# One gated-mix kernel: a bias loaded once, queries stacked in pairs of blocks, late masks moved to VectorE, and normalized tiles that land where they are split

## The chip, the cores and the metric

The kernel runs on one core of a Trainium2 chip. The metric is the device time in microseconds of one execution, the median of several. The profile names the engines PE (TensorE matmuls), PEld (its weight loads), DVE (VectorE), ACT (ScalarE), POOL (GpSimd) and SP (SyncE, which here issues every DMA).

## The reference, cut to what matters

The input `x` is 2048 rows of 512 floats. Three things are computed from it and mixed per row.

```
g = sigmoid((x * gate_w).sum(-1))                      # one number per row
a = attention(x): qkv = x @ wqkv, 32 heads of 16,      # row q sees rows q-255 .. q
    p = softmax(q.k / 4, masked), o = p @ v, a = o @ wo
b = gelu(x @ w1 + b1) @ w2 + b2                        # 512 -> 1792 -> 512
out = g * a + (1 - g) * b
```

## The kernel before, in words

All large products keep float32 accuracy by a split: each operand is a high part plus a low remainder, and `mm3` (lines 92 to 95) issues three 128x512 matmuls for one product. The high part of a tile is written by ACT (a copy into the F32R type), the remainder by DVE (a subtraction of that copy from the original).

**Order.** Nothing is scheduled by a tool. The program walks a hand-written loop, and `after(ns, fn)` puts later steps into a heap that is ordered by a virtual clock; `tick` advances that clock by each matmul's nominal length. So each engine's instructions stand in a fixed order which constants such as `LANDO`, `HOLD`, `HOLDO`, `NORM` and `DIV` set. At run time an engine works strictly down its list: an instruction that waits holds up everything behind it on that engine. SP issues all DMAs of the program from one such list, and each DMA signals on one of eight semaphores in turn, so a DMA's issue also waits until the one eight places earlier has landed.

**Stages.** First q, k and v are computed for four chunks of 512 rows and stored to DRAM. From then on two strands are interleaved on PE: the attention, and the dense part (MLP and then the output product) that fills the gaps. The attention goes through 8 groups of 4 heads; a group has 16 blocks of 128 keys, so there are 128 units (`u`). A unit that is 12 units ahead (`LEAD`) computes row maxima (`att_max`: matmul `sm` of `qd` and `kd`, L456; masked maximum on DVE, L461); `att_rows` turns four blocks' maxima into extra rows of the query tile `qs` by small POOL copies (`put`, L483). The unit itself computes scores (`st`, L500), exponentials on ACT (`pt`, L515) and clears the masked triangles of `pt` with POOL selects (L506, L509). After every fourth unit `att_pvs` multiplies the exponentials with v (L537): 98 small matmuls, which go through six blocks in pairs, the first pair being the first and the last block. A chunk's result `nd` is added up (L558 ACT, L561 DVE) and stored (L565).

**Stacking.** A tile such as `ks` or `qd` holds two heads' rows, one above the other, for alternating 64-wide column pieces. `ks` already uses pairs: the upper head takes the two middle pieces of every four, the lower head the two outer ones, so most runs are 128 elements long (three DMAs, L415, L410, L412). `qd` alternates single pieces of 64 elements (two DMAs, L429). `qs` receives whole rows (L436).

**Normalization.** For each chunk and each pair of groups `att_norm` loads the sums `den` (L575), takes reciprocals on DVE (L579), stores them (L582), loads them back spread over the heads as `rb` together with `num` (L587), multiplies on DVE (L591) and stores the tile `OT` (L594). `load_o` brings `OT` into a raw tile (L629), ACT writes the high part (L632), DVE the low part (L635), and `final` multiplies with `wo` (PE `a`, L93 to L95), mixes (L802) and stores the output (L807). Numbers behind a name give group or chunk: `nd7_1` is group 7, chunk 1; `num0_3` is chunk 0, pair 3 of groups.

**The bias.** In the first half of the MLP each output block starts from `b2`, loaded and spread over 128 rows by `ya_load` (L679), 16 times; in the second half it starts from the stored first half (L682).

Of the kernel before, what the change touches and what calls it, by code (L numbers as in the profile page):

```python
# [32 lines left out]
def gated_mix(ctx: ExitStack, tc: tile.TileContext, x, wqkv, wo, w1, b1, w2, b2, gate_w, out):  # L33
# [14 lines left out]
    idle = sb.tile([128, 384], BF16, tag="jm", bufs=1, name="idle")  # L48
# [20 lines left out]
    for r in (0, 64):  # L69
        nc.gpsimd.affine_select(out=mask[r:r + 64, 0:64], in_=mask[r:r + 64, 0:64], pattern=[[1, 64]],  # L70
                                compare_op=ALU.is_ge, fill=NEG, base=-1, channel_multiplier=-1)
        nc.gpsimd.affine_select(out=mask[r:r + 64, 256:320], in_=mask[r:r + 64, 256:320], pattern=[[-1, 64]],
                                compare_op=ALU.is_ge, fill=NEG, base=0, channel_multiplier=1)

# [243 lines left out]
    def warm(n):  # L318

        p = ps.tile([128, T], F32, tag="d", bufs=2, name=f"warm{now[0]}")  # L320
        for _ in range(n):
            nc.tensor.matmul(p[:, 0:384], idle[:, 0:128], idle, start=True, stop=True)
            tick(160)
# [76 lines left out]
    def load_ks(g_, c):  # L400


        ready(c, g_, 1)
        n = 2 * NB
        for s in range(2):
            v = f32(ks[64 * s + 4:64 * s + 52, slot(g_, c)]).rearrange("r a x -> r (a x)")
            src = part(SK[c], g_, s)
# [17 lines left out]
    def load_qd(g_, c):  # L425
        ready(c, g_, 0)
        for s in range(2):
            v = f32(qd[48 * s:48 * s + 48, slot(g_, c)]).rearrange("r a (n s j) -> r (a n) s j", s=2, j=64)[:, :, s]
            nc.sync.dma_start(v, part(SQ[c], g_, s).rearrange("r (n j) -> r n j", j=64))  # L429
# [37 lines left out]
    def att_rows(g_, rb):  # L467
# [11 lines left out]
        def put(i):  # L479
            r = 64 * (i // 2)  # L480
            dst = qs[r:r + 4, :, rb * RB * 128:(rb + 1) * RB * 128]
            dst = dst.rearrange("r s (b i j) -> r s b i j", b=2 * RB, i=2)[:, :, :, i % 2]
            nc.gpsimd.tensor_copy(dst, tt[32 * i:32 * i + 4].unsqueeze(1).broadcast_to([4, 2, 2 * RB, 32]))  # L483
            if i == 3:
                done.add(("rows", g_, rb))
        for i in range(4):
            after(PUT * (i + 1), put, i)

    def att_exp(g_, kb, i):
# [13 lines left out]
        def sel():  # L503
            for r in (0, 64):
                v = pt[r:r + 64]
                nc.gpsimd.affine_select(out=v[:, :, 0:64], in_=v[:, :, 0:64], pattern=[[0, 2], [1, 64]],  # L506
                                        compare_op=ALU.is_ge, fill=0.0, base=0, channel_multiplier=-1)
                if w == W + 64:
                    nc.gpsimd.affine_select(out=v[:, :, W:W + 64], in_=v[:, :, W:W + 64],  # L509
                                            pattern=[[0, 2], [-1, 64]], compare_op=ALU.is_ge, fill=0.0, base=-1,  # L510
                                            channel_multiplier=1)
# [9 lines left out]
    def att_pvs(u):  # L521
# [38 lines left out]
        def ev():  # L560
            nc.vector.tensor_add(nd, nd, pv[1])  # L561
            after(HOLD, store)

        def store():
            nc.sync.dma_start(ND[c][g_ // 2][g_ % 2], nd)  # L565
            done.add(("nd", g_, c))
            if g_ % 2 == 1:
                after(NORM, att_norm, c, g_ // 2)
        after(100, half), after(700, ev)

    def att_norm(t, c):

        v = ND[t][c].rearrange("g (i r) c -> (g i) r c", r=32)
        den = sb.tile([128, 32], F32, tag="den", bufs=2, name=f"den{t}_{c}")
# [21 lines left out]
        for ns, fn in zip(DIV, (rcp, keep, back, mul, store)):  # L596
# [16 lines left out]
    def load_o(t, cs=range(NC)):  # L613
# [8 lines left out]
        for c in cs:  # L622
            need(("o", t, c))
            if t == 0:
                raw = sb.tile([128, T], F32, tag=("x1", "raw")[c % 2], bufs=2, name=f"or{t}_{c}")
            else:
                raw = sb.tile([128, 2, 320], F32, tag="pt", bufs=PTS, name=f"or{t}_{c}")
                raw = raw.rearrange("p a b -> p (a b)")[:, 0:T]
            nc.sync.dma_start(raw, OT[t][c])  # L629

            def hi(c=c, raw=raw):
                nc.scalar.activation(ot[c][:, 0], raw, AF.Copy)  # L632

            def lo(c=c, raw=raw):
                nc.vector.tensor_sub(ot[c][:, 1], raw, f32(ot[c][:, 0]))  # L635
                done.add(("ot", t, c))
            n = cs.index(c)
            land = LAND if t == 0 else LANDO
# [33 lines left out]
    def ya_load(k):  # L672
# [3 lines left out]
        half, t = TURNS[n]  # L676
        yas[k] = ya = sb.tile([128, D], F32, tag="ya", bufs=2, name=f"ya{t}_{half}{b}")
        if half == 0:
            nc.sync.dma_start(ya, b2.partition_broadcast(128))  # L679
# [98 lines left out]
    def final(t):  # L778
# [3 lines left out]
        for b in range(NB):  # L782
# [8 lines left out]
            for k in range(n):  # L791
# [16 lines left out]
                after(100, ev), after(100 + HOLDO, store)  # L808
# [35 lines left out]
    for u in range(-LEAD, NU):  # L844
# [39 lines left out]
WARM = (7, 3)  # L884
# [16 lines left out]
LANDO = 5000.0  # L901
HOLD = 4000.0
HOLDQ = 1500.0
HOLDO = 1200.0
DIV = (6000, 9000, 12000, 18500, 22000)
# [26 lines left out]
```

## Time and profile before

| | |
|---|---|
| three timed runs | 787.20, 788.38, 788.43 us (median 788.38) |
| profiled execution | 788.64 us, span of its instructions 786.9 us |
| mean granted TensorE clock | 0.985 |
| busy share | PE 95%, DVE 65%, ACT 55%, POOL 55% |
| DMA | 176.07 MB in 203950 packets; 87.9% of sixteen engines' span |

The span runs from the first to the last instruction. A share of the whole span mixes the stages: up to about 110 us only q, k and v are computed, from 110 to about 735 us attention and MLP are interleaved, and from 735 us only the output product is left. The rows the argument rests on stand in the prediction.

### The profile page before, as it was taken

How to read it: one execution, taken by the hardware profiler on the slowest of the kernel's cores; microseconds unless marked ns; L12 is line 12 of the kernel's file. 1: busy time of each engine (PE TensorE's matmuls, PEld its weight loads, DVE VectorE, ACT ScalarE, POOL GpSimd, SP SyncE). 2: the span in 40 equal slices, each digit the busy share in tenths (PEclk: the TensorE clock that was granted, in tenths of full speed). 3: DMA queues.
4: the chain of work that ended last, by engine and by line, in shares of the span. 5: the costliest groups of instructions: out<-in, count | busy, mean ns of one | idle time of the engine just before them, and what ended most of it. 6: DMA issues, size and time to landing. Idle time of an engine off the chain costs nothing. (4 is left out here: it accounts for less than half of the span.)

```text
span 786.9 us, 18205 instructions
## 1 busy us (share of the span) xinstructions
PE 747.3 (95%) x6102; PEld 616.2 (78%) x6102; DVE 510.5 (65%) x1548; ACT 432.9 (55%) x973; POOL 431.3 (55%) x1129
## 2 busy tenths in 40 slices
PE   8999999979999999999999999999999999977988
PEld 6888887757888887887878777888888888765767
DVE  3532326869758867875897689678758966722434
ACT  4434433249448734854784577458547845943442
POOL 3200000219867964886797679768758966963100
PEclk9999999989999999999999999999999999988999
DMA  9979899998996899899878999996999998347563
GB/s 280 369 250 362 293 349 296 239 282 180 258 252 148 195 244 208 191 205 259 196 170 183 218 241 215 242 228 116 223 226 237 199 246 221 70 109 212 193 234 110
DMA packets 203950, 176.07 MB, mean 224 GB/s; under 512 B 102480, under 2 KB 145744, under 8 KB 203856
## 3 DMA queue, kind: packets, MB, share of 16 engines
q1 hardware_dynamic: 203856, 174.90, 87.9%
q8 instruction: 48, 0.79, 0.5%
q14 instruction: 46, 0.38, 0.2%
HBM read 112.47 MB, written 62.39 MB: 222 GB/s over the span
## 5 line engine op out<-in xcount | busy, mean ns | idle before, releaser
L461 DVE CUSTOM_DVE_ANT_0 jm<-sm,mask 128x320 bf16<-128x320 f32 (+4 forms) x512 | 238.1, 465 | 72.9 <-PE sm L456 44.4
L515 ACT ACTIVATE pt<-st 128x320 f32<-128x320 f32 (+4 forms) x512 | 206.4, 424 | 130.2 <-PE st L500 126.7
L506 POOL TENSOR_SCALAR_AFFINE_SELECT pt<-pt 64x128 f32<-64x128 f32 x512 | 182.6, 357 | 153.7 <-ACT pt L515 131.9
L509 POOL TENSOR_SCALAR_AFFINE_SELECT pt<-pt 64x128 f32<-64x128 f32 x448 | 167.3, 373 | 0.0
L456 PE MATMUL sm<-kd,qd 96*128 96x320 f32 (+4 forms) x512 | 157.3, 310 | 9.9 <-DMA ya<-in_B_b_dram 4.9
L500 PE MATMUL st<-qs,ks 128*128 128x320 f32 (+4 forms) x512 | 156.1, 309 | 7.0 <-ACT pt L515 7.0
L456 PEld LDWEIGHTS sm<-kd,qd 96*128 96x128 f32 x512 | 96.6, 189 | 39.5 <-DVE M L461 15.8
L500 PEld LDWEIGHTS st<-qs,ks 128*128 128x128 f32 x512 | 97.8, 191 | 27.4 <-ACT pt L515 8.7
L483 POOL CAST qs<-tt 4x512 fp32r<-4x512 f32 x128 | 88.4, 691 | 35.3 <-DVE tt L477 16.2
L93 PE MATMUL y<-w,h 128*128 128x512 f32 x224 | 90.7, 405 | 0.0
L94 PE MATMUL y<-w,h 128*128 128x512 f32 x224 | 88.6, 395 | 0.0
L95 PE MATMUL y<-w,h 128*128 128x512 f32 x224 | 88.3, 394 | 0.0
L537 PE MATMUL pv_sm<-pt,vbuf 64*32 64x320 f32 (+4 forms) x1408 | 82.5, 366 | 5.6 <-DVE M L461 3.5
L537 PE MATMUL pv_st<-pt,vbuf 64*32 64x320 f32 (+4 forms) x1408 | 80.9, 366 | 6.7 <-POOL pt L506 3.9
L93 PE MATMUL u<-mx,w 128*128 128x512 f32 x196 | 80.1, 409 | 0.0
L537 PEld LDWEIGHTS pv_sm<-pt,vbuf 64*32 64x32 f32 x1408 | 60.0, 112 | 23.7 <-DVE M L461 6.3
L94 PE MATMUL u<-mx,w 128*128 128x512 f32 x196 | 77.3, 394 | 0.0
L95 PE MATMUL u<-mx,w 128*128 128x512 f32 x196 | 77.1, 393 | 0.0
L537 PEld LDWEIGHTS pv_st<-pt,vbuf 64*32 64x32 f32 x1408 | 54.1, 112 | 7.6 <-POOL pt L506 4.2
L299 POOL MEMSET vx<- 128x32 f32 x16 | 2.5, 156 | 93.1 <-DMA SK<-qke 32.0
L280 DVE TENSOR_TENSOR qke<-qk,qke 128x512 fp32r<-128x512 f32 x32 | 22.1, 690 | 46.6 <-ACT qke L277 36.6
L95 PEld LDWEIGHTS y<-w,h 128*128 128x128 f32 x224 | 42.3, 189 | 10.0 <-DVE h L665 0.2
(140 smaller groups left out, 1341.3 us busy)
## 6 DMA issues: line engine op xcount, KB each, us to landing
kd<-SK SPq DMA_DIRECT2D x32, 384.0 KB
qd<-SQ SPq DMA_DIRECT2D x64, 192.0 KB
qs<-SQ SPq DMA_DIRECT2D x64, 192.0 KB
mx<-XT SPq DMA_DIRECT2D x24, 512.0 KB
SQ<-qke SPq DMA_DIRECT2D x16, 512.0 KB
SK<-qke SPq DMA_DIRECT2D x16, 512.0 KB
ND<-nd SPq DMA_DIRECT2D x32, 256.0 KB
raw_w<-in_B_w_dram SPq DMA_DIRECT2D x28, 256.0 KB
```

Of the source, the lines that this page charges most:

```text
L93: nc.tensor.matmul(p, lh, rh, start=first, stop=False)
L94: nc.tensor.matmul(p, lh, rl, start=False, stop=False)
L95: nc.tensor.matmul(p, ll, rh, start=False, stop=last)
L280: nc.vector.tensor_sub(e[:, 1 - h], p, f32(e[:, h]))
L456: nc.tensor.matmul(p[:, :w], qd[0:96, n, pr, 128 * j:128 * (j + 1)], kd[0:96, n, pr, k1 - w:k1], start=True, stop=True)
L461: nc.vector.tensor_tensor_reduce(junk[:, :w], p[:, :w], mask[:, 320 - w:320], 1.0, -3e38, ALU.add, ALU.max, M[:, 2 * (b % RB) + hb, pr:pr ...
L483: nc.gpsimd.tensor_copy(dst, tt[32 * i:32 * i + 4].unsqueeze(1).broadcast_to([4, 2, 2 * RB, 32]))
L500: nc.tensor.matmul(p[:, :w], ks[:, slot(g_, kb // NB), pr, at:at + 128], qs[:, pr, k0:k0 + w], start=True, stop=True)
L506: nc.gpsimd.affine_select(out=v[:, :, 0:64], in_=v[:, :, 0:64], pattern=[[0, 2], [1, 64]], compare_op=ALU.is_ge, fill=0.0, base=0, channel ...
L509: nc.gpsimd.affine_select(out=v[:, :, W:W + 64], in_=v[:, :, W:W + 64], pattern=[[0, 2], [-1, 64]], compare_op=ALU.is_ge, fill=0.0, base=- ...
L515: nc.scalar.activation(pt[:, pr, :w], p[:, :w], AF.Exp, scale=SCALE)
L537: nc.tensor.matmul(pv[r // 64][32 * i:32 * i + 32, q - c * T:e - c * T], vts[g_, b // NB][r:r + 64, v:v + 32], rhs(r), start=start, stop=s ...
```

## The change

Five things change.

1. `b2` is loaded once; the one tile serves all sixteen blocks.
2. `qd` is stacked in pairs like `ks`, through a shared `put_pairs`: three DMAs a load instead of two, with runs of 128 elements in place of 64. The query rows that `put` writes follow the new stacking, so each of its copies is cut in two (256 of 256 elements a row in place of 128 of 512).
3. In the last 12 units the masks are one DVE minimum with a constant tile `cut` (3e38 where a value is kept, zero where it is masked) per half block, in place of two or four POOL selects.
4. `load_o` loads `OT` straight into the low half of the tile that is split; ACT reads it there and DVE overwrites it. The raw tiles fall away; the load itself now waits until the tile's former user is done.
5. Delays: the first query loads `load_qs(0, ...)` come at every fourth unit, `LAND0` is 13500 for the first chunk's split (7500 before), `LANDO` 6500 (5000), `HOLDO` 3000 (1200), and the last two normalizations use shorter delays. The warm-up matmuls are 9 of 320 columns in place of 7 of 384.

The core of the diff:

```diff
+    cut = cp.tile([128, 2, 64], F32, name="cut")
+    nc.gpsimd.memset(cut, 3e38)
...
+        put_pairs([f32(ks[64 * s + 4:64 * s + 52, slot(g_, c)]) for s in range(2)], SK[c], g_)
+
+    def put_pairs(to, st, g_):
...
     def load_qd(g_, c):
         ready(c, g_, 0)
-        for s in range(2):
-            v = f32(qd[48 * s:48 * s + 48, slot(g_, c)]).rearrange("r a (n s j) -> r (a n) s j", s=2, j=64)[:, :, s]
-            nc.sync.dma_start(v, part(SQ[c], g_, s).rearrange("r (n j) -> r n j", j=64))
+        put_pairs([f32(qd[48 * s:48 * s + 48, slot(g_, c)]) for s in range(2)], SQ[c], g_)
...
-            nc.gpsimd.tensor_copy(dst, tt[32 * i:32 * i + 4].unsqueeze(1).broadcast_to([4, 2, 2 * RB, 32]))
...
+            src = tt[32 * i:32 * i + 4].rearrange("r (b h) j -> r b h j", h=2)[:, :, hb]
+            nc.gpsimd.tensor_copy(dst, src.unsqueeze(1).broadcast_to([4, 2, RB, 32]))
...
+            if g_ * NKB + kb >= NU - LEAD:
+                v = pt.rearrange("p a (e x) -> p a e x", x=64)[:, :, 0:4 * n - 3:4]
+                nc.vector.tensor_tensor(v, v, cut[:, 0:n].unsqueeze(1).broadcast_to([128, 2, n, 64]), op=ALU.min)
...
-            after(HOLD, store)
+            after(HOLD if g_ * NT + c < NQ - 2 else 800, store)
...
-                after(NORM, att_norm, c, g_ // 2)
+                after(NORM if g_ * NT + c < NQ - 2 else 3500, att_norm, c, g_ // 2)
...
-        for ns, fn in zip(DIV, (rcp, keep, back, mul, store)):
+        for ns, fn in zip(DIVS[c == NC - 1 and t >= NT - 2], (rcp, keep, back, mul, store)):
...
-            nc.sync.dma_start(raw, OT[t][c])
+            nc.sync.dma_start(f32(ot[c][:, 1]), OT[t][c])
...
-                nc.scalar.activation(ot[c][:, 0], raw, AF.Copy)
+                nc.scalar.activation(ot[c][:, 0], f32(ot[c][:, 1]), AF.Copy)
...
-            land = LAND if t == 0 else LANDO
+            land = LAND0 if t == 0 else LANDO
...
+        if half == 0 and k:
+            yas[k] = xts["b2"]
+            return
...
-        if QAT <= m < QAT + NT - 1:
-            load_qs(0, m - QAT)
-        if m == QAT + NT:
-            load_qs(0, NT - 1)
+        if m % NB == QAT % NB and QAT <= m < QAT + NKB:
+            load_qs(0, (m - QAT) // NB)
...
-LANDO = 5000.0
+LAND0 = 13500.0
+LANDO = 6500.0
...
-HOLDO = 1200.0
-DIV = (6000, 9000, 12000, 18500, 22000)
+HOLDO = 3000.0
+DIVS = ((6000, 9000, 12000, 18500, 22000), (4500, 5700, 8500, 13500, 15000))
```

Where the order moves, the changed file's own line numbers stand in the rows. First, VectorE near the end of the attention, around the normalization of chunk 0; before the change:

```order
L733 SCALAR_TENSOR_TENSOR yo_10623<-y3_11_10571,ya3_11_9962 128x512
L591 TENSOR_TENSOR num0_3_10642<-num0_3_10642,rb0_3_10644 128x512
L579 RECIPROCAL den1_3_10659<-den1_3_10659 128x32
L635 TENSOR_TENSOR ot0_10661<-or0_0_10662,ot0_10661 128x512
L635 TENSOR_TENSOR ot0_10661<-or0_1_10664,ot0_10661 128x512
L635 TENSOR_TENSOR ot0_10661<-or0_2_10666,ot0_10661 128x512
L561 TENSOR_TENSOR nd7_2_10774<-nd7_2_10774,pv7_2_sm_10720 128x512
```

The same place with the change (L520 is the new minimum, L607 the multiply, L646 the low part of a split):

```order
L748 SCALAR_TENSOR_TENSOR yo_10722<-y3_11_10679,ya3_11_10092 128x512
L607 TENSOR_TENSOR num0_3_10738<-num0_3_10738,rb0_3_10740 128x512
L595 RECIPROCAL den1_3_10752<-den1_3_10752 128x32
L520 TENSOR_TENSOR pt7_11_1_10749<-pt7_11_1_10749,cut_151 128x2x2x64
L520 TENSOR_TENSOR pt7_12_0_10777<-pt7_12_0_10777,cut_151 128x2x2x64
L577 TENSOR_TENSOR nd7_2_10851<-nd7_2_10851,pv7_2_sm_10797 128x512
L646 TENSOR_TENSOR ot0_10754<-ot0_10754 128x512 x2
```

The three splits of chunk 0 have moved from ahead of the sum `nd7_2` to behind it, and the mask of the last block of group 7's third chunk (`pt7_11_1`) now stands on VectorE behind the multiply of `num0_3`.

Second, the DMA list of SP around the first query loads of the attention, before the change:

```order
L436 DMA qs_174<-SQ1_71 48x2x512 x2
L145 DMA raw_w20_1545<-in_B_w2_dram 128x512
L284 DMA SK3_77<-qke3_6_1535 128x2x512
L285 DMA SK3_77<-qke3_6_1535 128x512
L436 DMA qs_174<-SQ2_72 48x2x512 x2
L423 DMA kd_177<-SK2_76 96x2x256
L423 DMA kd_177<-SK3_77 96x2x512
L429 DMA qd_176<-SQ3_73 48x16x64 x2
```

And with the change (L428, L423 and L425 are the three DMAs of a paired load, L436 is now `kd`):

```order
L153 DMA raw_w20_1558<-in_B_w2_dram 128x512
L292 DMA SK3_77<-qke3_6_1548 128x2x512
L293 DMA SK3_77<-qke3_6_1548 128x512
L436 DMA kd_183<-SK2_76 96x2x256
L436 DMA kd_183<-SK3_77 96x2x512
L428 DMA qd_182<-SQ3_73 48x8x128
L423 DMA qd_182<-SQ3_73 48x7x128
L425 DMA qd_182<-SQ3_73 48x2x64
```

The four loads of `qs` for chunks 1 and 2, which stood ahead of the maxima's `kd` and `qd` for chunk 3, now come later, and one `qd` load is three DMAs with longer runs.

More of the change, by code (lines that the diff above doesn't have):

```diff
@@ L46, in f32 @@
         return ap.bitcast(F32)
-    idle = sb.tile([128, 384], BF16, tag="jm", bufs=1, name="idle")
+    idle = sb.tile([128, 320], BF16, tag="jm", bufs=1, name="idle")
     nc.gpsimd.memset(idle, 0.0)
@@ L321, in warm @@
         for _ in range(n):
-            nc.tensor.matmul(p[:, 0:384], idle[:, 0:128], idle, start=True, stop=True)
-            tick(160)
+            nc.tensor.matmul(p[:, 0:320], idle[:, 0:128], idle, start=True, stop=True)
+            tick(134)
     def qkv(t):
@@ L573, in att_norm @@
         v = ND[t][c].rearrange("g (i r) c -> (g i) r c", r=32)
-        den = sb.tile([128, 32], F32, tag="den", bufs=2, name=f"den{t}_{c}")
+        den = sb.tile([128, 32], F32, tag="den", bufs=1, name=f"den{t}_{c}")
         nc.sync.dma_start(den, v[:, 16, :].rearrange("i (j c) -> i j c", c=32))
@@ L807, in store @@
                     nc.sync.dma_start(out[nb * 128:(nb + 1) * 128, cs], a[:, cs])
-                after(100, ev), after(100 + HOLDO, store)
+                after(100, ev), after(100 + (HOLDO if nb < NT * NB - 2 else 800), store)
     later = [("w1", i) for i in range(HF)] + [("w2", i) for i in range(HF)]
```

51 lines of the change are left out of this document (27 added, 24 removed).

## The prediction

> **What bounds the kernel now.** I read the page's busy shares first, then PE's waits, then windows around them.
>
> ```profile
> PE 747.3 (95%) x6102; PEld 616.2 (78%) x6102; DVE 510.5 (65%) x1548; ACT 432.9 (55%) x973; POOL 431.3 (55%) x1129
> DMA packets 203950, 176.07 MB, mean 224 GB/s; under 512 B 102480, under 2 KB 145744, under 8 KB 203856
> q1 hardware_dynamic: 203856, 174.90, 87.9%
> ```
>
> PE works 95% of the span and the change takes no matmul of the product away, so all it can win lies in the 39.6 us in which PE idles and in matmuls that ran at a lowered clock. The DMA engines, 88% busy, are the second resource. Who ended PE's waits, in us, times, longest:
>
> ```profile
> PE st L500 <- ACT pt L515: 7.0, 4, 5.5
> PE sm L456 <- DMA ya<-in_B_b_dram: 4.9, 1, 4.9
> PE pv_st L537 <- POOL pt L506: 3.9, 2, 3.4
> PE a L93 <- DVE ao L802: 3.5, 2, 2.0
> ```
>
> Four places make up half of the idle time: one at the attention's start, two in its last chunks, one in the output product. Windows (length, busy PE, PEld, DVE, ACT, POOL, then the granted clock, DMA share, GB/s) show what comes on top:
>
> ```profile
> 166.00:175.00 9.00, 5.49 (x18) 4.79 (x19) 6.22 (x19) 4.84 (x10) 0.82 (x2) 0.62 0.91 320
> 624.80:627.50 2.70, 2.70 (x98) 2.11 (x97) 2.34 (x9) 1.03 (x2) 2.53 (x7) 1.00 1.11 241
> 689.90:698.70 8.80, 5.19 (x98) 3.67 (x97) 1.54 (x3) 1.65 (x4) 5.38 (x16) 0.65 0.07 11
> 717.20:722.30 5.10, 4.96 (x98) 3.57 (x97) 0.00 (x0) 0.51 (x2) 1.83 (x7) 0.50 0.69 182
> 732.10:735.60 3.50, 3.00 (x99) 2.23 (x97) 0.69 (x1) 0.95 (x2) 0.79 (x3) 1.00 0.19 57
> 735.50:787.00 51.50, 44.59 (x210) 36.56 (x204) 21.79 (x34) 17.32 (x28) 0.00 (x0) 1.00 0.53 180
> ```
>
> The same 98 matmuls of `att_pvs` take 2.7 us at full clock (group 6, chunk 1) and 8.8 us for group 7, chunk 1, where a wait of 3.4 us was followed by half clock. For chunk 2 they take 5.1 us at half clock behind a wait of 5.5 us. Waits of that length are paid for twice.
>
> **The change part by part.** Sums are made against the profiled execution (span 786.9, time 788.64, so 1.7 us lie around the span; its time is 0.3 above the median of 788.38).
>
> *The attention's start.* The wait, a window around it, SP's list (start, length) and the sizes:
>
> ```profile
> 169.51 0.64 PE L456 MATMUL sm<-kd,qd 96*128 96x320 f32 x1 [4.94 <-DMA ya<-in_B_b_dram]
> 164.00:170.00 6.00, 1.06 (x5) 0.62 (x4) 1.50 (x4) 2.30 (x4) 0.00 (x0) 0.75 1.01 271
> 154.49 2.15 SPq L436 DMA_DIRECT2D qs<-SQ  x2
> 156.73 0.97 SPq L423 DMA_DIRECT2D kd<-SK  x2
> 157.75 1.01 SPq L429 DMA_DIRECT2D qd<-SQ  x2
> 164.28 2.08 SPq L679 DMA_DIRECT2D ya<-in_B_b_dram  x2
> qd<-SQ SPq DMA_DIRECT2D x64, 192.0 KB
> ya<-in_B_b_dram SPq DMA_DIRECT2D x16, 256.0 KB
> ```
>
> The wait of 4.9 us is named after `ya`, but the matmul reads `kd` and `qd`, issued at 156.7 to 158.8 and, if the last of them ended the wait at 169.5, landed some 11 us later: the DMA queue is backed up, its engines busy throughout (1.01). Four `qs` loads of 192 KB that stood ahead now come later: 0.79 MB at the 320 GB/s of the window are 2.5 us. Four paired `qd` loads stand ahead or are the awaited one: 1536 runs each become 816. For a run's price I have two bounds: at one price per byte nothing is won; at the mean price per packet, 0.879 x 786.9 x 16 / 203856 = 54 ns, 4 x 720 x 54 / 16 ns = 9.7 us. I take a third, 3.2 us, because half-length packets cannot cost as much as the mean of all. 2.5 + 3.2 = 5.7 exceeds 4.9, so the wait goes, and with it the low clock: 9.00 x (1 - 0.62) = 3.4 us, less the 1.2 of it that fall into the wait (6.00 x 0.25 = 1.5 up to 170.0). **-7.1**, bounds -2.5 (the `qs` loads alone) and -7.1.
>
> The Trainium skill ("DMA: Bandwidth & Descriptors", section "Specifications") says that transfers under 512 B miss line rate, because the engine reads, modifies and writes. By that rule halving the number of runs pays, and the sum is the -17.7 below; were bytes the only price, this term would be -2.5 and the sum -13.1. No row of this profile tells the two apart.
>
> *The rest of the DMA relief.* Fifteen loads of `b2`, 3.9 MB, at the mean 224 GB/s are 17.6 us of queue time; 28 more `qd` loads bring 0 to 68 (at 54 ns a run). Neither is on PE's path as such. What it shortens are VectorE's waits for `rb`:
>
> ```profile
> L591 DVE TENSOR_TENSOR num<-num,rb 128x512 f32<-128x512 f32 x16 | 11.2, 701 | 22.2 <-DMA rb<-RD 21.0 <-issue 1.3
> 300.00:450.00 150.00, 144.16 (x1349) 121.01 (x1348) 114.98 (x371) 93.55 (x213) 107.94 (x283) 0.99 0.91 205
> ```
>
> PE idles 5.8 us in this window. I take **-1.5** for the whole middle, bounds 0 and -6. SP gets 32 - 15 = 17 issues more of about 0.5 us; it waits far more than it issues.
>
> *The masks of the last chunks.* A DVE operation on two tiles of 128x512 floats takes 0.69 us (713.61 in the rows below), a minimum over half as many about 0.36, and one replaces four selects. For chunk 1 the wait goes, 8.8 - 2.7 = 6.1; VectorE gets eight minima (3 us) among GELU steps, so I keep 0.5 of delay: **-5.6**, bounds -3 and -6.1.
>
> *Chunks 2 and 3* have another cause, and the price is worked out from chunk 1's end (698.7):
>
> ```profile
> 700.05 0.34 DVE L579 RECIPROCAL den<-den 128x32 f32<-128x32 f32 x1
> 700.18 0.44 ACT L515 ACTIVATE pt<-st 128x320 f32<-128x320 f32 x1 [0.76 <-PE st L500]
> 703.60 0.61 SPq L587 DMA_DIRECT2D rb<-RD  x1
> 713.61 0.69 DVE L591 TENSOR_TENSOR num<-num,rb 128x512 f32<-128x512 f32 x1 [4.34 <-DMA rb<-RD]
> 714.22 2.07 ACT L632 ACTIVATE ot<-or 128x512 fp32r<-128x512 f32 x3 [5.06 <-DMA or<-OT]
> 716.67 0.63 PE L500 MATMUL st<-qs,ks 128*128 128x320 f32 x1 [5.45 <-ACT pt L515]
> 730.01 0.69 DVE L591 TENSOR_TENSOR num<-num,rb 128x512 f32<-128x512 f32 x1 [3.08 <-DMA rb<-RD]
> ```
>
> Before, ACT stood at the split `ot<-or`, waiting for its DMA, and the exponentials queued behind it. Now that split comes behind chunk 2's product, and ACT is free. But the product's first pair needs the mask of block 11, which stands on VectorE behind the multiply `num`, and that waits for `rb`: 713.61, 14.9 after chunk 1's end. It even comes 0.9 later, since the reciprocal now stands behind a mask that needs the exponential of 700.18. So chunk 2 can start at 14.9 + 0.9 + 0.7 (multiply) + 0.35 + 0.36 = 17.2. PE arrives at 711.2 - 698.7 = 12.5 plus 0.3 for a score, 12.8, and waits 4.4: longer than the 3.4 us that halved the clock at chunk 1, so the 5.1 us of before again: end at 22.3 (before 23.6). The next multiply follows 16.4 after the first (730.01 - 713.61), at 32.2; behind it stand three masks, a `yo` and the mask of block 15: 0.7 + 0.7 + 4 x 0.2 = 2.2, so 34.4. PE arrives 9.8 (732.1 - 722.3) after 22.3, at 32.1, and waits 2.3. With 2.7 - 0.3 for the product, the output product starts 36.8 after chunk 1's end: before 735.5 - 698.7 = 36.8. **0**: the ACT wait is exchanged for a VectorE wait. Bounds: -8.8 if the multiply is never late (12.8 + 2.7 + 9.8 + 2.7 = 28.0), +4 if both waits halve the clock.
>
> *The output product:*
>
> ```profile
> 761.92 0.23 PE a L94
> 754.23 0.50 PE L93 MATMUL a<-wo,ot 128*128 128x512 f32 x1 [2.04 <-DVE ao L802]
> 751.60 1.90 DVE L635 TENSOR_TENSOR ot<-or,ot 128x512 fp32r<-128x512 f32 x3 [0.96 <-ACT ot L632]
> 745.70 1.35 SPq L629 DMA_DIRECT2D or<-OT  x3
> 750.93 1.84 ACT L632 ACTIVATE ot<-or 128x512 fp32r<-128x512 f32 x3 [8.83 <-DMA or<-OT]
> ```
>
> VectorE stood at a split whose tile had not landed, the mix `ao` behind it came late, and PE found no free PSUM. Later splits (`LANDO`) and output stores that no longer hold up SP (`HOLDO`) take both waits away: **-3.5**, bounds 0 and -3.5. The new condition, that `OT` of chunk 2 may land only when chunk 0's product is done, leaves chunk 1's product, 48 matmuls of 0.23 us = 10.9 us, for a load that took 5.2 (745.70 to 750.93) and four subtractions (2.8): hidden by 2.9; without that cover, 1 to 2 us.
>
> *Costed at nothing:* `put` and the warm-up.
>
> ```profile
> L483 POOL CAST qs<-tt 4x512 fp32r<-4x512 f32 x128 | 88.4, 691 | 35.3 <-DVE tt L477 16.2 <-PE sm L456 11.9
> 8.19 0.50 PE L93 MATMUL qk<-ks,qk 128*128 128x512 f32 x1 [0.72 <-ACT qk L153]
> ```
>
> Twice as many copies of half the size cost POOL between 0 and 88 us more in all, 0 to 2.8 us for each set of four that becomes eight; POOL is 55% busy and the rows are made some units ahead of their use, which covers it. Without that cover each of 32 sets could delay scores by up to 2.8. The warm-up (some 0.2 us longer) ends in a wait for ACT.
>
> Sum: -7.1 - 1.5 - 5.6 + 0 - 3.5 = -17.7; span 769.2, time **770.9**.
>
> **The rivals.**
>
> *VectorE's multiply is in time* (0.22). The DMA queue, with 23040 fewer of 102480 small packets, brings `rb` before PE arrives at chunks 2 and 3. For it: `rb` was issued 10 us before it landed, so queueing is most of it. Against it: the bytes ahead of it in this stretch (`YB`, `num`, 2 KB rows) are unchanged. -17.7 - 8.8 = -26.5: 762.1.
>
> *The queue is not relieved* (0.15). Run length is no price, or another transfer takes the place of the awaited one, and output waits reappear elsewhere: -2.5 at the start, 0 in the middle, -5.6, +2 at chunks 2 and 3, 0 at the end: -6.1, 782.5. This is also the case in which the change does not do what it says.
>
> *SP becomes the bound* (0.05), slower than before. Each paired load puts a third DMA, of 24 KB only, into the list, and every issue waits for the landing of the one eight places earlier; in the backlog two issues took 2.15 us (154.49). If each of the 32 loads holds SP a further 1.1 us and `kd`, `qd` reach PE that much later, 35 - 9.1 (masks and output product) = +26, 814; it decides from the point at which SP's lead over PE is used up, and only what exceeds 9.1 makes the kernel slower. Against it: of the four waits listed above only the one at 169.5 is for such a load. The Trainium skill ("DMA: Bandwidth & Descriptors", section "Bandwidth") calls transfers under 64 KB dominated by their descriptors, which speaks for this rival; it measured loads issued by GpSimd, and no run here shows it yet.
>
> **How the numbers follow.** Forecast 0.58, rivals 0.22, 0.15, 0.05. The time is the forecast's, 771. Its own range is 765 to 777, from the bounds at the start, for the masks and at chunks 2 and 3; with most of the in-time case and of the unrelieved one it becomes 761 to 783. Differences under 0.2%, 1.6 us, cannot be told from none; the unrelieved case ends there at times: faster 0.92, same 0.03, slower 0.05.
>
> **What would show it.** The page of the changed kernel should show about 46000 fewer packets under 512 B (`qd`'s 32 x 1536 runs become 32 x 816, of which 96 each stay short) and DMA share below 88%; PE's wait for `sm` at 165 to 170 gone; chunk 1's 98 matmuls in under 3.5 us; at chunk 2 a PE wait of 3 to 5 us with VectorE at `num` before it; no wait of `a` for `ao`. A PE wait for POOL in the last 100 us, or for `kd` or `qd` in the middle, would prove me wrong; so would chunk 2 without a wait, in the other direction.

## The result and the profile after

The changed kernel takes 778.14 us (median of 775.01, 777.76, 778.52 and 778.56), the kernel before 787.79 us beside it. The ratio is 0.9872 with a 95% interval of 0.9841 to 0.9903: 1.3% faster, 9.7 us. The forecast was 771, in a range of 761 to 783. The profiled execution took 778.52 us, with a span of 776.8. One execution of `e11_v` below took 1015.32 us at a mean granted clock of 0.655, a slow state that is in neither its median nor its ratio.

The rows of the changed kernel's page that answer to those shown of before: busy shares, DMA packets, the DMA queue.

```profile
PE 744.8 (96%) x6104; PEld 615.8 (79%) x6104; DVE 515.9 (66%) x1572; ACT 431.6 (56%) x973; POOL 424.6 (55%) x1174
DMA packets 179262, 172.14 MB, mean 222 GB/s; under 512 B 56672, under 2 KB 122976, under 8 KB 179168
q1 hardware_dynamic: 179168, 170.97, 83.4%
```

The runs under 512 B fell by 45808, as forecast, and the DMA engines' share from 87.9 to 83.4%. PE still idles 32 us. Who ended its waits (us, times, longest):

```profile
PE pv_st L553 <- POOL pt L525: 4.4, 5, 1.7
PE sm L467 <- DVE M L472: 3.7, 7, 1.0
PE pv_st L553 <- issue: 3.5, 1, 3.5
PE a L101 <- DVE ao L817: 3.1, 2, 2.3
PE pv_st L553 <- DVE pt L520: 2.3, 1, 2.3
```

In the first row the waits for POOL's masks have moved. The kernel before had three at `pv_st`, two at L506 (3.9 us, in the prediction) and one at L509:

```profile
PE pv_st L537 <- POOL pt L509: 1.3, 1, 1.3
```

The longest of these, 3.4 us, was the chunk 1 of group 7 that the masks were moved for. After the change there are five, none of them in the last 100 us. Windows around the same places as before (columns as there), the three middle ones being the products of chunks 1, 2 and 3 of group 7:

```profile
166.00:175.00 9.00, 6.85 (x30) 5.30 (x31) 8.04 (x26) 6.54 (x15) 4.76 (x11) 0.97 1.10 288
...
687.59:690.07 2.48, 2.48 (x97) 2.05 (x96) 2.29 (x5) 1.62 (x4) 0.00 (x0) 1.00 0.17 24
702.33:709.88 7.55, 4.00 (x97) 2.92 (x96) 1.56 (x4) 0.44 (x1) 0.00 (x0) 0.81 0.61 177
719.54:724.47 4.93, 2.61 (x98) 2.03 (x96) 2.36 (x7) 1.35 (x3) 0.00 (x0) 1.00 0.63 220
724.47:776.80 52.33, 46.03 (x211) 37.68 (x204) 21.95 (x35) 17.08 (x28) 0.00 (x0) 0.97 0.53 177
```

Split at the products (each stage ends where the next matmul starts), in us:

| stage | before | after | change | forecast |
|---|---|---|---|---|
| up to the first attention product | 190.5 | 187.4 | -3.1 | -7.1 |
| the middle, up to the end of group 7, chunk 0 | 486.2 | 486.4 | +0.2 | -1.5 |
| to the end of chunk 1 | 22.0 | 16.2 | -5.7 | -5.6 |
| chunks 2 and 3 | 36.8 | 34.4 | -2.4 | 0 |
| output product | 51.4 | 52.3 | +0.9 | -3.5 |
| span | 786.9 | 776.8 | -10.1 | -17.7 |

One warning for what follows. Eight kernels here (the changed one and runs `e2`, `e4`, `e7`, `e8`, `e10`, `e11`, `e12` below) have the same middle, and in their single profiles it takes from 483.3 to 488.6 us. So a stage of one profile speaks for a cause only where a wait or a product shows it; whole kernels are compared by ratios, whose intervals are some 0.25 to 0.45% to each side.

### The profile page after: what moved, and what is told of

The parts are those of the page before. It is cut to its first block, busy times and chain, and to the rows that moved or that the text cites. A ratio compares the mean times of both kernels' runs of the same rounds, so it can differ in the third digit from the quotient of the medians.

```text
span 776.8 us, 18309 instructions
## 1 busy us (share of the span) xinstructions
PE 744.8 (96%) x6104; PEld 615.8 (79%) x6104; DVE 515.9 (66%) x1572; ACT 431.6 (56%) x973; POOL 424.6 (55%) x1174
## 3 DMA queue, kind: packets, MB, share of 16 engines
q1 hardware_dynamic: 179168, 170.97, 83.4%
## 4 chain that ended last, share of the span: by engine, by line
PE 65%; DMA 13%; POOL 6%; DVE 6%; issue 3%; SPq 3%; ACT 3%; DVEq 0%; ACTq 0%; POOLq 0%
PE sm L467 7%; PE st L513 6%; PE pv_sm L553 6%; POOL pt L525 5%; DMA rb<-RD 5%; PE y L101 5%; PE u L101 4%; PE y L103 4%; PE y L102 4%; PE u L103 4%; PE u L102 4%; PE qk L101 4%; PE qk L103 3%; PE qk L102 3%; PE v L101 2%
## 5 line engine op out<-in xcount | busy, mean ns | idle before, releaser
L525 POOL TENSOR_SCALAR_AFFINE_SELECT pt<-pt 64x128 f32<-64x128 f32 x872 | 294.1, 357 | 102.7 <-ACT pt L531 82.0
L495 POOL CAST qs<-tt 4x256 fp32r<-4x256 f32 x256 | 116.9, 457 | 39.1 <-DVE tt L488 15.6
L553 PE MATMUL pv_st<-pt,vbuf 64*32 64x320 f32 (+4 forms) x1408 | 76.8, 355 | 12.2 <-POOL pt L525 4.4
L553 PE MATMUL pv_sm<-pt,vbuf 64*32 64x320 f32 (+4 forms) x1408 | 78.7, 355 | 2.4 <-DVE M L472 1.2
L553 PEld LDWEIGHTS pv_sm<-pt,vbuf 64*32 64x32 f32 x1408 | 56.3, 108 | 19.9 <-DVE M L472 3.1
L553 PEld LDWEIGHTS pv_st<-pt,vbuf 64*32 64x32 f32 x1408 | 50.5, 108 | 13.4 <-POOL pt L525 7.3
L574 ACT ACTIVATE nd<-pv_st 128x512 f32<-128x512 f32 x32 | 19.1, 597 | 57.5 <-PE pv_sm L553 53.4
```

The lines of the kernel that those rows point to most:

```text
L495: nc.gpsimd.tensor_copy(dst, src.unsqueeze(1).broadcast_to([4, 2, RB, 32]))
L525: nc.gpsimd.affine_select(out=v, in_=v, pattern=[[0, 2], [1 - 2 * e, 64]], compare_op=ALU.is_ge, fill=0.0, base=-e, channel_multiplier=2 * ...
L553: nc.tensor.matmul(pv[r // 64][32 * i:32 * i + 32, q - c * T:e - c * T], vts[g_, b // NB][r:r + 64, v:v + 32], rhs(r), start=start, stop=s ...
L574: nc.scalar.activation(nd, pv[0], AF.Copy)
```

## The experiments

Each run changes the kernel after the change, unless it says otherwise; all ratios are to the kernel before, timed beside it on the same chip. As a yardstick: the change itself is 0.9872.

| run | what | median, us | ratio, 95% interval |
|---|---|---|---|
| `e1_single` | `qd` in single pieces again | 779.20 | 0.9898 (0.9852 to 0.9943) |
| `e2_poolmask` | last masks on POOL again | 783.75 | 0.9960 (0.9933 to 0.9987) |
| `e3_split` | kernel before, row copies cut in two | 791.75 | 1.0050 (1.0022 to 1.0078) |
| `e4_chunk1` | VectorE masks for chunk 1 only | 775.89 | 0.9863 (0.9819 to 0.9908) |
| `e5_qs` | first `qs` loads where they were | 783.43 | 0.9947 (0.9921 to 0.9972) |
| `e6_b2` | `b2` loaded sixteen times | 781.88 | 0.9918 (0.9887 to 0.9949) |
| `e7_land` | `LANDO`, `HOLDO` as before | 774.58 | 0.9847 (0.9806 to 0.9888) |
| `e8_mul` | three multiplies on POOL | 772.21 | 0.9805 (0.9776 to 0.9834) |
| `e10_raw` | `e4`, own buffers for the last `nd` | 776.94 | 0.9866 (0.9831 to 0.9902) |
| `e11_v` | `e10`, last v loaded early | 777.34 | 0.9869 (0.9824 to 0.9914) |
| `e12_all` | `e11`, two multiplies on POOL | 774.95 | 0.9835 (0.9794 to 0.9876) |
| `e14_dve` | `e12`, chunk-1 masks on VectorE in all groups | 766.56 | 0.9742 (0.9703 to 0.9780) |

**The middle: what the paired stacking gives and takes.** Two runs separate its two halves, the shorter DMA queue and the smaller POOL copies. The first takes both back, the second puts the smaller copies alone into the kernel before.

```diff
 e1_single
-        put_pairs([f32(qd[48 * s:48 * s + 48, slot(g_, c)]) for s in range(2)], SQ[c], g_)
+        for s in range(2):
+            v = f32(qd[48 * s:48 * s + 48, slot(g_, c)]).rearrange("r a (n s j) -> r (a n) s j", s=2, j=64)[:, :, s]
+            nc.sync.dma_start(v, part(SQ[c], g_, s).rearrange("r (n j) -> r n j", j=64))
...
+            nc.gpsimd.tensor_copy(dst, tt[32 * i:32 * i + 4].unsqueeze(1).broadcast_to([4, 2, 2 * RB, 32]))
 e3_split (on the kernel before)
-            nc.gpsimd.tensor_copy(dst, tt[32 * i:32 * i + 4].unsqueeze(1).broadcast_to([4, 2, 2 * RB, 32]))
+            src = tt[32 * i:32 * i + 4].rearrange("r (b h) j -> r b h j", h=2)[:, :, hb]
+            nc.gpsimd.tensor_copy(dst, src.unsqueeze(1).broadcast_to([4, 2, RB, 32]))
```

> The changed kernel with one part undone: qd is stacked in single pieces of 64 again (two DMAs a load) and each row copy on POOL is whole again (4 of 512 elements in place of 8 of 256). Theory (in the middle, the smaller copies on POOL cost as much as the shorter DMA queue gives): POOL copies about 690 ns each, 88 us in all, in place of 117; the chunk-1 products of groups 0, 3 and 4 take 2.9 to 3.2 us again in place of 4.6, 4.6 and 6.2; the wait of about 5 us for kd, qd at the attention's start and PE's waits behind longer rb waits return; the middle stays within 2 us of 486.3, the start is 2 to 4 us longer, so 780 to 783 us in all. Rival (the row copies do not matter, the DMA relief is simply worth little): the products of chunk 1 stay at 4.5 us and more, and the whole is within 1 us of 778.1, or 3 us up at the start alone. Rival (the paired loads cost more than they give): 774 or less.

> The kernel before with one thing changed: each row copy on POOL is cut into two of half the size (8 of 256 elements in place of 4 of 512), same stacking and same DMAs as before. Theory (the smaller copies are what lengthens chunk 1's products in the middle): copies of about 457 ns, 117 us in all; the chunk-1 products of several groups take 1 to 3 us longer than the 2.6 to 3.1 us of before, and the whole is 3 to 9 us above the kernel before. Rival (POOL has room for the copies; the products of the changed kernel are longer for another reason): within 1 us of the kernel before, products unchanged.

The product of group 3, chunk 1, shows it in one window of each trace. After the change, then `e3_split`, `e1_single`, and `e14_dve`, of which more below:

```profile
408.89:413.47 4.58, 2.90 (x96) 2.15 (x96) 3.33 (x10) 0.95 (x2) 4.22 (x12) 1.00 0.98 188
```

```profile
416.34:420.92 4.58, 2.90 (x97) 2.15 (x97) 3.33 (x10) 1.07 (x3) 4.25 (x13) 1.00 1.26 193
```

```profile
410.42:413.48 3.06, 2.71 (x96) 2.12 (x96) 2.78 (x9) 0.95 (x2) 2.83 (x8) 1.00 1.28 218
```

```profile
406.68:409.10 2.42, 2.42 (x96) 1.99 (x96) 1.78 (x7) 0.87 (x2) 1.75 (x5) 1.00 1.23 189
```

PE's work is about the same each time; the rest is waiting while POOL (the fifth pair of numbers) works without a pause. With small copies the window is 4.58 us, whatever the stacking (4.58 to 6.28 in the eight kernels of the same middle); with whole copies it is 3.06, and before the change it was 3.07. Groups 4 and 6 go the same way (6.23 and 3.74 us after the change, 3.06 and 2.58 in `e1_single`), group 5 by 0.3 only. POOL's copies in the changed kernel (count, busy time, mean ns of one) and its list ahead of that window (start, length):

```profile
L495 POOL CAST qs<-tt 4x256 fp32r<-4x256 f32 x256 | 116.9, 457 | 39.1 <-DVE tt L488 15.6
...
376.77 3.86 POOL L495 CAST qs<-tt 4x256 fp32r<-4x256 f32 x6
380.70 1.59 POOL L525 TENSOR_SCALAR_AFFINE_SELECT pt<-pt 64x128 f32<-64x128 f32 x4
382.35 0.40 POOL L495 CAST qs<-tt 4x256 fp32r<-4x256 f32 x1
382.81 12.63 POOL L525 TENSOR_SCALAR_AFFINE_SELECT pt<-pt 64x128 f32<-64x128 f32 x28
395.50 3.29 POOL L495 CAST qs<-tt 4x256 fp32r<-4x256 f32 x6
```

There is no idle entry in 25 us. A copy of half the size takes 457 ns where the whole took 691, so the split adds 116.9 - 88.4 = 28.5 us of POOL work, and it lands in stretches in which POOL is behind. Alone it costs 0.50% (0.22 to 0.78), 4 us, of which the middle of its one profile shows 3.1 (489.3 against 486.2). `e1_single` came out where the changed kernel is, within the intervals, so the two halves cancel: the stacking as a whole is worth nothing that can be measured. My own expectation for `e1_single` was wrong about the start, which did not get longer (186.5); so the whole stayed just under the 780 to 783 us that I expected. The middle, 484.0 us, is also 0.3 below what I allowed. The product of group 0, chunk 1, is an exception that I can't explain: 6.51 us, where the eight kernels with small copies and the same middle show 3.8 to 6.3. Why the start was not longer is what the next two runs ask.

**The start.**

```diff
 e5_qs
-        if m % NB == QAT % NB and QAT <= m < QAT + NKB:
-            load_qs(0, (m - QAT) // NB)
+        if QAT <= m < QAT + NT - 1:
+            load_qs(0, m - QAT)
+        if m == QAT + NT:
+            load_qs(0, NT - 1)
 e6_b2
-        if half == 0 and k:
+        if half == 0 and k < 0:
```

> The changed kernel with one part undone: the four first query loads (load_qs of group 0) stand at units 5, 6, 7 and 9 again in place of every fourth unit. The run with single stacking still had its first attention product at 186.5, so the paired loads did not free the start. Theory (the query loads that stood in front of kd and qd did): the first product starts at 190 to 192 in place of 187.4 and PE waits 3 us or more for sm near 165 to 170; in all 780 to 783 us. Rival (the sixteen loads of b2, which the wait was named after): first product at 186 to 188, in all within 1 us of 778.

> The changed kernel with b2 loaded sixteen times again (256 KB each). Theory (the b2 load in front of kd and qd held up the start): first product at 190 to 192 in place of 187.4, a wait of 3 us or more for sm near 165 to 170, in all 780 to 783 us; the rest of the middle moves by less than 1 us. Rival (the place of the query loads): first product at 186 to 188, in all within 1 us of 778.

With the `qs` loads back, the first product starts at 190.6 (before 190.5, after 187.4), though `qd` is loaded in pairs and `b2` once. The wait came back whole, and the rows around it say what was awaited. `e5_qs`, by time:

```profile
167.67 0.63 ACT L161 ACTIVATE w<-raw_w 128x512 fp32r<-128x512 f32 x1 [8.12 <-DMA raw_w<-in_B_w_dram]
168.33 0.69 DVE L165 TENSOR_TENSOR w<-raw_w,w 128x512 fp32r<-128x512 f32 x1 [6.31 <-ACT w L161]
169.49 0.64 PE L467 MATMUL sm<-kd,qd 96*128 96x320 f32 x1 [5.33 <-DVE M L472]
```

The kernel before has the same chain; its PE row, shown in the prediction, is named after `ya`:

```profile
167.69 0.63 ACT L153 ACTIVATE w<-raw_w 128x512 fp32r<-128x512 f32 x1 [7.79 <-DMA raw_w<-in_B_w_dram]
168.36 0.69 DVE L157 TENSOR_TENSOR w<-raw_w,w 128x512 fp32r<-128x512 f32 x1 [5.74 <-ACT w L153]
```

And after the change:

```profile
164.44 0.63 ACT L161 ACTIVATE w<-raw_w 128x512 fp32r<-128x512 f32 x1 [3.43 <-DMA raw_w<-in_B_w_dram]
166.26 0.41 PE L467 MATMUL sm<-kd,qd 96*128 96x320 f32 x1 [0.66 <-DVE M L472]
```

So PE waited neither for `ya` nor for `kd` and `qd`, as I had it, but for a free buffer in PSUM, the memory that its matmuls write to. VectorE, whose masked maximum reads that buffer, could not empty it, because the remainder of a weight tile stood ahead in its list; that waits for ScalarE's high part, and that for the weight's DMA, which queues behind the `qs` loads. In all `e5_qs` is 5.9 us above the changed kernel by the ratios; the start explains 3.2 of it, and the rest lies within the intervals. `e6_b2` moved the start by 1.0 us only, so its theory failed although its time of 781.88 was met. Its 3.7 us over the changed kernel (the intervals overlap at their edges) fit the middle better: the product of group 1, chunk 3, takes 5.36 us there, 5.53 before and 2.37 after the change, and in front of it VectorE's multiply stands 1.2 us at `rb`.

**The last masks, and the link behind them.**

```diff
 e2_poolmask
-            if g_ * NKB + kb >= NU - LEAD:
+            if False:
 e4_chunk1
-            if g_ * NKB + kb >= NU - LEAD:
+            if NU - LEAD <= g_ * NKB + kb < NU - 8:
 e10_raw (e4_chunk1 and)
-        nd = sb.tile([128, T], F32, tag="tmp", bufs=3, name=f"nd{g_}_{c}")
+        late = g_ * NT + c >= NQ - 2
+        nd = sb.tile([128, T], F32, tag=("tmp", "raw")[late], bufs=3 - late, name=f"nd{g_}_{c}")
 e11_v (e10_raw and)
         vt = vbuf[:, c % 2]
+        if g_ * NT + c == NQ - 1:
+            vt = sb.tile([128, T], F32, tag="raw", bufs=2, name="vlast")[:, 0:NB * 68 + 16]
...
-                att_load_v(*divmod(u // NB, NT))
+            if u // NB < NQ - 1:
+                att_load_v(*divmod(u // NB, NT))
+            if u // NB == NQ - 2:
+                att_load_v(*divmod(NQ - 1, NT))
```

> The changed kernel with the masks of the last 12 units on POOL again (two or four selects in place of one minimum on VectorE). Theory (chunk 1 of group 7 waits for POOL, chunks 2 and 3 wait only because their masks stand behind VectorE's multiply, which waits for rb): chunk 1 takes 21 to 22 us in place of 16.2, with the product at 8 to 9 us; from its end to the start of the output product 28 to 29 us in place of 34.4, with no wait over 1 us in front of the two products; in all 776 to 779 us. Rival (chunks 2 and 3 wait for something that the masks only inherit, the exponentials or the DMA queue): 34 us stay, in all 783 to 785.

> The changed kernel with VectorE's masks for the four units of chunk 1 of group 7 alone; chunks 2 and 3, where POOL has no copies left to do, use POOL selects. Theory (POOL was late in chunk 1 only; later its masks are in time and those on VectorE wait behind the multiply): chunk 1 stays at 16 to 17 us, then 28 to 29 us in place of 34.4 to the start of the output product, in all 771 to 774 us. Rival (the wait of chunks 2 and 3 goes to another engine when VectorE is taken out, as it did from ScalarE to VectorE): 33 to 36 us, in all 777 to 780.

> The kernel with POOL masks for chunks 2 and 3, and one thing more: the results nd of chunks 2 and 3 of group 7 get buffers of their own (those of the weights' raw tiles, free by then) instead of taking turns with num and rb. In the run before ScalarE stood 5.65 us at chunk 2's nd until the store of num had landed, and PE waited behind it. Theory (that buffer was the last link that tied chunk 3 to rb): no wait over 1 us from chunk 2's product to the output product, 28 to 29.5 us from chunk 1's end to there in place of 33.2, in all 770 to 773 us. Rival (a further link takes over again): 32 to 34 us, in all 774 to 777.

> The kernel with POOL masks for chunks 2 and 3 and own buffers for their nd, and one thing more: v of the last chunk is loaded together with that of the chunk before, into a buffer of its own. In the run before, SyncE issued this load at 710.4, behind the store of num that waited for rb, and PE waited 6.8 us for it at chunk 3. Theory (the list of SyncE was the link that tied chunk 3 to rb): no wait over 1 us in front of chunk 3's product, 28 to 29.5 us from chunk 1's end to the output product in place of 35.8, in all 768 to 771 us; the output product may get up to 2 us of it back as waits, since its tiles still come through rb. Rival (another link takes over once more): 33 us or more, in all 774 to 778.

In us:

| | chunk 1 | its product | chunks 2 and 3 | their products | output product |
|---|---|---|---|---|---|
| after | 16.2 | 2.48 | 34.4 | 7.56, 4.94 | 52.3 |
| `e2_poolmask` | 22.5 | 9.30 | 31.9 | 2.32, 3.79 | 52.1 |
| `e4_chunk1` | 16.2 | 2.49 | 33.2 | 2.32, 5.05 | 53.4 |
| `e10_raw` | 16.2 | 2.49 | 35.8 | 2.32, 11.57 | 49.5 |
| `e11_v` | 16.2 | 2.49 | 27.8 | 2.32, 3.41 | 61.3 |

The masks on VectorE are what frees chunk 1, 6.3 us of it. In chunk 2 they stand behind the multiply, as the changed kernel's rows show (the profile names no releaser for PE's wait, hence "issue"; PE went on at 706.17, when the first of the two masks was done):

```profile
704.84 0.69 DVE L607 TENSOR_TENSOR num<-num,rb 128x512 f32<-128x512 f32 x1 [4.41 <-DMA rb<-RD]
705.45 0.35 DVE L595 RECIPROCAL den<-den 128x32 f32<-128x32 f32 x1
705.71 0.69 DVE L520 TENSOR_TENSOR pt<-pt,cut 128x256 f32<-128x256 f32 x2
706.17 0.25 PE L553 MATMUL pv_st<-pt,vbuf 64*32 64x64 f32 x2 [3.55 <-issue]
```

With POOL masks chunk 2 goes at once (2.32 us), but the rivals were right about the rest: each freed wait came back one link further on. `e2_poolmask` kept waits of 1.3 us at a score and 1.2 at chunk 3's product, so 31.9 us and not 28 to 29. Its chunks 1 to 3 add up to 3.8 us over the changed kernel, its ratio to 6.9, which is the rival's number. The rest has no cause in the edit: 2.2 us of it is the middle of this one profile (488.6), which the edit does not touch, and the intervals of the two ratios would allow 3.8. In `e4_chunk1` it was a buffer, ScalarE at chunk 2's `nd`, whose slot the store of `num` had to leave:

```profile
706.13 0.60 ACT L574 ACTIVATE nd<-pv_st 128x512 f32<-128x512 f32 x1 [5.65 <-DMA OT<-num]
...
706.78 0.42 PE L513 MATMUL st<-qs,ks 128*128 128x320 f32 x1 [1.87 <-ACT nd L574]
```

In `e10_raw`, with a buffer of its own, it was SyncE's list. The load of v for chunk 3 stands behind that store, went out at 710.37 and reached PE at 718.68:

```profile
703.21 0.32 SPq L611 DMA_DIRECT2D OT<-num  x1
710.37 0.56 SPq L453 DMA_DIRECT2D vbuf<-SV  x1
718.68 0.32 PE L553 MATMUL pv_st<-pt,vbuf 64*32 64x64 f32 x2 [6.83 <-DMA vbuf<-SV]
```

In `e11_v` the attention ended as expected, 27.8 us after chunk 1, and the output product took it all back: 61.3 us, with waits of 3.4, 1.2 and 3.2 us and a mean clock of 0.89. Its tiles come through the same `rb`. The whole was not faster (0.9869).

**The output product.**

```diff
 e7_land
-LANDO = 6500.0
+LANDO = 5000.0
-HOLDO = 3000.0
+HOLDO = 1200.0
 e8_mul
-            nc.vector.tensor_mul(num, num, rb)
+            (nc.gpsimd if c == NC - 1 and t else nc.vector).tensor_mul(num, num, rb)
 e12_all (e11_v and)
+            (nc.gpsimd if c == NC - 1 and t >= NT - 2 else nc.vector).tensor_mul(num, num, rb)
```

> The changed kernel with LANDO 5000 and HOLDO 1200 as before, all else as changed. The forecast's view (later splits and later output stores take PE's waits out of the output product): the product takes 54 to 56 us in place of 52.3 and the whole 780 to 782. Theory now (those waits come from VectorE's multiply that stands at rb, which the two constants do not move): 51.5 to 54 us, the whole within 1.5 us of 778.

> The changed kernel with the multiply of num and rb moved from VectorE to POOL for the last three chunks of the last pair of groups; the masks stay on VectorE. Theory (the masks of chunks 2 and 3, and the mix ao in the output product, wait only because VectorE stands at the multiply for rb): chunk 2's product of 98 matmuls takes 2.3 to 2.6 us in place of 7.6; chunk 2's result on ScalarE then still waits for the buffer that the multiply's store frees, as in the run with POOL masks, so 33 to 34 us stay from chunk 1's end to the output product; the output product, 52.3 us, loses its wait of 2.3 us for ao and takes 49 to 50.5; in all 774 to 777 us. Rival (ao and the masks wait for the DMA queue by other ways): chunk 2 stays above 5 us or the output product above 51.5; in all 777 to 780.

> The same with the multiplies of num and rb for the last two chunks of the last pair of groups on POOL, which has no masks left by then. Theory (VectorE's multiply holds up ao in the output product, as the run with three multiplies on POOL showed with 47.6 us): the output product takes 47.5 to 49.5 us, in all 764 to 768 us. Rival (with chunk 3 earlier the tiles themselves, not VectorE, are late): 50 us or more, in all 767 to 771.

Undoing the two delays cost nothing: the output product takes 50.3 us, below the 51.5 to 54 I expected, and the ratio of 0.9847 is some 2 us under the changed kernel's, with overlapping intervals. What the product gained on the changed kernel's 52.3 us is mostly the granted clock: 1.00 over the product, against 0.97 there, with a mean of 0.83 between 735 and 745. The wait in the changed kernel stands behind the same kind of multiply:

```profile
735.20 0.69 DVE L607 TENSOR_TENSOR num<-num,rb 128x512 f32<-128x512 f32 x1 [4.12 <-DMA rb<-RD]
735.80 1.29 DVE L646 TENSOR_TENSOR ot<-ot 128x512 fp32r<-128x512 f32 x2
737.01 0.75 DVE L817 SCALAR_TENSOR_TENSOR ao<-a,g,ao 128x512 f32<-128x512 f32 x1
737.67 1.29 DVE L646 TENSOR_TENSOR ot<-ot 128x512 fp32r<-128x512 f32 x2
737.90 0.76 PE L101 MATMUL a<-wo,ot 128*128 128x512 f32 x1 [2.26 <-DVE ao L817]
```

With the multiplies on POOL (`e8_mul`) the output product takes 47.6 us, less than the 49 to 50.5 expected, and PE has no wait over 0.3 us in it; POOL stands at `rb` instead, and nobody queues behind it:

```profile
735.96 1.30 POOL L607 TENSOR_TENSOR num<-num,rb 128x512 f32<-128x512 f32 x1 [13.68 <-DMA rb<-RD]
...
724.50:772.10 47.60, 44.26 (x214) 36.65 (x204) 21.34 (x33) 17.10 (x28) 2.59 (x2) 0.99 0.58 195
```

Chunk 2's wait only fell to 2.45 us there, and its product took 6.56 us, not the 2.3 to 2.6 I had written, because the multiply in front of its masks is that of chunk 0, which this edit left on VectorE. In `e12_all`, where chunk 3 is earlier by the links cut above, another multiply left on VectorE, that of chunk 1, stood ahead of a remainder that the output product needs; behind it a reciprocal then waited for its own load, and PE stood 4.4 us:

```profile
722.11 0.69 DVE L611 TENSOR_TENSOR num<-num,rb 128x512 f32<-128x512 f32 x1 [11.32 <-DMA rb<-RD]
...
725.56 0.35 DVE L599 RECIPROCAL den<-den 128x32 f32<-128x32 f32 x1 [2.16 <-DMA den<-ND]
725.83 0.63 DVE L650 TENSOR_TENSOR ot<-ot 128x512 fp32r<-128x512 f32 x1
726.51 0.80 PE L103 MATMUL a<-wo,ot 128*128 128x512 f32 x1 [4.43 <-DVE ot L650]
```

The output product takes 53.4 us, as its rival said; the whole, 774.95, is above what either expected. By these rows, moving that multiply alone need not have been enough, since the reciprocal's wait came after it.

**POOL in the middle, relieved.**

```diff
 e14_dve (e12_all and)
-            if NU - LEAD <= g_ * NKB + kb < NU - 8:
+            if NU - LEAD <= g_ * NKB + kb < NU - 8 or kb in (6, 7):
```

> The same, and in every group the masks of blocks 6 and 7, the last two of chunk 1, as minima on VectorE. Theory (in the middle chunk 1's products wait for POOL, which runs without a pause there; a set of row copies puts it behind): those products take 2.3 to 3 us in groups 0 and 3 to 6, in place of 3.4 to 6.2, in all 6 to 10 us less than with POOL masks, 755 to 761. Rival (VectorE, busy throughout in these stretches, turns late in POOL's place and holds up the maxima): the products shorten, but PE waits as much for sm and M; in all 763 to 768 or more.

The products of chunk 1 in groups 0 and 3 to 6 fell to 3.25, 2.43, 2.71, 2.36 and 2.43 us (the window of group 3 stands above, 2.42), PE's waits for POOL at `pv_st` to 0.4 us in one, while PE's waits behind VectorE's maxima moved from 3.7 to 2.6 us at `sm` and from 1.6 to 2.8 at `pv_sm`. The median is 8.4 us under that of `e12_all`, and the middle takes 479.5 us in its profile, below all eight of before (483.3 to 488.6), so the theory's gain came. The whole is higher than I wrote, and in the rival's range, because `e12_all` was higher. At 0.9742 it beats both kernels. `e8_mul`'s three multiplies together with these masks, without `e10_raw` and `e11_v`, were not tried.

## Why the prediction was right and wrong

The time fell in the range, but the sum was 17.7 us where 10.1 came, and only one of its five terms was right with its reason. That the range held it is luck in part: 778.1 lies outside the 765 to 777 of the sum's own bounds, and the top of the stated range came from a rival that did not happen.

*Start: -7.1, measured -3.1.* The size that survives is the lower bound, the `qs` loads alone: 2.5 estimated, 3.2 by `e5_qs`. The failed step is "the matmul reads `kd` and `qd`": PE waited for a buffer behind a weight's split, so the `qd` loads' run length was not on the path (`e1_single` starts at 186.5 with single pieces). The low clock did not go either, though the window shows 0.97 in place of 0.62: it moved. Three short waits (0.66, 1.03 and 0.86 us) came in place of the long one, and from 174.5 to 178.0 the granted clock was 0.51, where before it was 1.00 from 174 to 178; that is 1.7 us of work lost just behind the window.

The price of a run can be given: between `e1_single` and the changed kernel the DMA share of the span falls from 86.5 to 83.4% with 22528 packets fewer, (0.865 x 776.6 - 0.834 x 776.8) x 16 / 22528 = 17 ns for each, a third of the mean price of 54, as I had taken it. It is good to some 4 ns, since the kernel before and `e3_split`, with the same DMAs, differ by 4.9 us of DMA time (87.9% of 786.9 and 86.7% of 792.1) where these two differ by 23.9. In direction this agrees with the Trainium skill's rule that transfers under 512 B miss line rate ("DMA: Bandwidth & Descriptors", section "Specifications"). Fewer, longer runs do free the queue; who gains by it is another question.

*Middle: -1.5, measured +0.2.* The failed step is the one costed at nothing, "POOL is 55% busy ... which covers it". A share of the span hid that POOL is behind in chunk 1 of most groups; there the copies cost 4 us (`e3_split`) and ate what the DMA relief gave, such as the product of group 1, chunk 3, that fell from 5.53 to 2.37 us. I had listed a PE wait for POOL as proof against me, but looked for it only in the last 100 us, where none came.

*Chunk 1: -5.6, measured -5.7.* Right, and `e2_poolmask` gives 6.3 for it.

*Chunks 2 and 3: 0, measured -2.4.* The mechanism was right: the ACT wait became a VectorE wait behind the multiply. The multiply came 14.8 us after chunk 1's end, where the sum had 14.9 + 0.9 = 15.8: the reciprocal was late as said, but `rb` came 9.1 us after its issue and not 10.0. So the product could go on 16.1 us after chunk 1's end and not 17.2, which is 1.1 us of the 2.4, and PE waited 3.55 us and not 4.4. The other mis-sized term is the half clock. After the wait the product took 3.7 us and not 5.1, because the clock was still full when PE went on: it was granted 0.82 from 706.17 to 707.50 and 0.50 only from there to 709.88. Before, behind a wait of the same length (3.45 us) at chunk 1, it had been at 0.50 already when PE went on. So the length of the wait does not settle when the clock falls, and what does is not shown here. What I did not see is how many links tie these chunks to `rb`: engine, buffer and SyncE's list, one behind the other.

*Output product: -3.5, measured +0.9.* The failed step is that later splits and stores "take both waits away". `e7_land` shows that they do nothing measurable here. PE's two waits for `ao` only went from 3.5 to 3.1 us, so the sign "no wait of `a` for `ao`" failed. The plus of 0.9 goes with the granted clock of 0.97 in place of 1.00, some 1.6 us of 52.3. The split that had stood at its tile was gone, but the multiply that stands at `rb` was ahead of `ao` too, and `e8_mul` shows that it is the cause: 47.6 us.

*The rivals.* SyncE as the bound did not happen: no long wait of PE is for `kd` or `qd`. The Trainium skill's rule that transfers under 64 KB are dominated by their descriptors ("DMA: Bandwidth & Descriptors", section "Bandwidth") spoke for it, and no run here shows its cost. The unrelieved queue came nearest in time (782.5) but for a wrong reason: the queue was relieved, and POOL's smaller copies spent it.

## What to carry to other kernels

Before moving work to an engine, look at its busy share in the stretch where the work will land, not over the span; 55% may be 100% for 25 us at a time. Behind a wait in a strict list, ask what else depends on the awaited transfer (engine, buffer, DMA list), since cutting one link alone only moved the wait here; moving the instruction that waits to an engine with nothing behind it (`e8_mul`, 0.9805) did more than cutting three (`e11_v`, 0.9869; the intervals just overlap). And follow a wait named after a DMA back through the engines: the name is that of the last event, not of the cause.

## What the runs showed of the hardware that I had not expected

- Half a POOL copy costs two thirds: 457 ns for 4x256 against 691 for 4x512, so about 0.9 ns for an element of a row and 220 ns for each instruction.
- POOL multiplies two 128x512 float tiles in 1.26 to 1.30 us, VectorE in 0.70; where the engine has nothing else to do, that is cheap.
- A run of 256 B saved by joining two into one of 512 is worth 17 ns of one DMA engine, a third of the mean packet's time.
- The same wait does not cost the same: behind 3.45 us the granted clock was 0.50 from the first matmul on, behind 3.55 us it fell 0.9 us later, and in the changed kernel's start two waits of 1.03 and 0.86 us were followed by 3.5 us at 0.51.
